# Block-recurrent cross-attention and a cosine-gated feed-forward: moving weight conversion into the middle of a step, evictions to ScalarE, and the order of the first steps

## The chip, the cores and the metric

The kernel runs on one core of a Trainium2 chip. The metric is the device time of one execution in microseconds (us); lower is better. The profiled execution that is quoted below is one of these executions, recorded by the hardware profiler. Its engines are called PE (TensorE), DVE (VectorE), ACT (ScalarE), POOL (GpSimd) and SP (SyncE, which here only issues DMAs).

## The reference, cut to what matters

The inputs are `x` (8, 8, 512, 64), `state` (8, 8, 32, 64), `w_in` (512, 2048) and `w_out` (2048, 512). The two weights arrive as float64, all else as float32.

```
scores  = x @ state.T / 8;  a  = softmax(scores)     # per batch b and head h
xread   = a @ state                                  # (512, 64) per head
scores2 = state @ x.T / 8;  a2 = softmax(scores2)
sread   = a2 @ x                                     # (32, 64) per head
X = concat([xread, sread], axis=2)  ->  (8 * 544, 512), heads side by side
h = X @ w_in                                         # (4352, 2048)
out = (h * cos(h)) @ w_out                           # (4352, 512)
```

## The kernel before

**Steps.** The main loop runs over tiles, one tile a step: for each batch b of 8, sixteen tiles f of 128 hidden columns by 512 tokens, and then sixteen tiles for the state rows of all batches together, 144 steps in all. Step s of batch 0 is called step s below. The order on each engine is the order of the program text, since the schedule is written out by hand (`manual_schedule`); the engines wait for each other's results.

**What a step does.** `hidden(t)` (L440) makes the hidden tile on PE: two products in float32, recorded as four matmul rows of 128x512. The attention output is never formed: `hidden` multiplies the normalised scores `aT` by `sw`, the product of the state and `w_in` ("state products", `products`, L410, one 512-column quarter nt of `w_in` at a time, evicted from PSUM to `sw` by `products_kept`, L415). The state is scaled by 1/2pi, so that the cosine is taken of 2pi h. `gate` (L446, ACT) adds a magic number that rounds, `gate2` (L451, DVE) takes the distance from the rounded value, `gate3` (L456, ACT) does Abs and Sin, `gate4` (L461, DVE) multiplies by h into `g_all` and so frees the PSUM buffer of the hidden tile. There are two such buffers, so `hidden(t+2)` waits for `gate4(t)`. `output` (L583, by `product`, L506) multiplies g by a block of `w_out`, some steps later (`LAG`): tile t-4 in steps below 8, tile t-3 from step 8 on, where two outputs are done in one step.

**The second product in seven parts.** For two batches together `w_out` is used as a 2x2 block matrix with sums and differences (`s1` to `s4`) made on POOL by `blocks` (L774) in steps 15 to 23; sums and differences of g tiles are made by `minus` (L468) on POOL or DVE.

**The weights' conversion.** Each load of 1 MB of float64 (18 of them, 0 to 3 half as large) is converted in six parts (`convert`, L201): "1" and "2" on ACT read the high and the low words (L218, L221), "a" limits from below (L225, DVE), "b" shifts left (L227, DVE), "c" puts in the sign (L230, DVE), "d" adds the low words (L240, POOL) and, from load 4 on, is split into two instructions of 128x512. Part "c" also sends the next load on SP's queue (`fetch`), since the raw words have been read. Conversion i is begun in the step that `conv_at` (L770) gives: parts "1", "2", "a", "b" there, "a" and "b" behind `gate4`; and "c", "d" in the next step between `gate2` and `gate4`. Loads 4, 5, 7, 8, 10, 11 are `w_in`, 6, 9, 12, 13 the upper half of the blocks of `w_out` and 14 to 17 the others; conversions 4 to 12 stand in steps 0 to 8 and 13 to 17 in steps 10 to 14.

**Where the attention stands.** `plan` (L707) puts the attention of batch b+1 into the steps of batch b, in four lists: `x_act` and `x_dve` are worked off between `gate2` and `gate3`, `y_act` and `y_dve` behind `gate4`. `early` places the transposes of x, the scores, the two maxima (`max1`, `max2`), the shift, both exponentials (`exps`), the sums and the norm; `late` the transposes and products of the state's reads, with `keep`. In steps 0 to 15 `plan(0)` places what is left of batch 0, the state products of batch 0, and the attention of batch 1. `late` and `keep` stand in step 3 for batch 0 and in step 14 for batch 1.

**The start.** Before step 0 (L674 to L702) the first loads, batch 0's attention and conversions 0 to 3 are done; seven products of zeros (`warm`, L668) stand behind the scores. `conv_at`, `plan` and `last` in the loop (L800: conversion 3's "cd" in step 0) set the rest.

The lines that set the order in a step:

```
        hidden(t); go(0)                      # PE: the hidden tile, then plan's products
        gate(t); gate2(t); go(1); go(3)       # x_act, x_dve
        if last >= 0: convert(last, "cd")     # of the step before
        if conv >= 0 and not todo[1]: convert(conv, "1")
        gate3(t); ...; gate4(t)
        ...
        if conv >= 0: convert(conv, "2")
        go(4)                                 # y_dve
        if conv >= 0: convert(conv, "ab")
        ...output...
```

Of the kernel before, what the change touches and what calls it, by code (L numbers as in the profile page):

```python
# [10 lines left out]
I32 = mybir.dt.int32  # L11
U32 = mybir.dt.uint32
ALU = mybir.AluOpType
# [10 lines left out]
def kernel(  # L24
# [8 lines left out]
    nc = tc.nc  # L33
# [9 lines left out]
    WC = 512  # L43
# [24 lines left out]
    NH = NF // 2  # L68
# [50 lines left out]
    def load_state(half, queues):  # L119
        b = slice(4 * half, 4 * half + 4)  # L120
        for k in range(NK):
# [11 lines left out]
    acc = [[ops.tile([P, S], F32, name=f"o{m}{ch}") for ch in range(2)]  # L133
           for m in range(2)]
# [16 lines left out]
    HC = WC // 2  # L151
# [49 lines left out]
    def convert(i, parts):  # L201

        if i < len(loads) and f64:
            for p in parts:
                convert_part(i, p)
        if "c" in parts and i not in (1, 2) and i + 3 < N_LOADS:
            fetch(max(i + 4, 6))

    def convert_part(i, p):
        raw, dst = raws[i], loads[i][0]
        bits = dst.bitcast(I32)
        m, w = dst.shape[1:]
        c0 = m * w if i in (2, 3) else 0
        e = low[i % 2][:, c0:c0 + m * w].rearrange("p (m f) -> p m f", m=m)
        if p == "1":
            nc.scalar.activation(dst, raw.bitcast(F32)[:, :, :, 1],  # L218
                                 func=ACTF.Abs)
        elif p == "2":  # L220
            nc.scalar.activation(e, raw.bitcast(U32)[:, :, :, 0],  # L221
                                 func=ACTF.Copy, scale=2.0 ** -51, bias=2.0)
        elif p == "a":
            engine = nc.gpsimd if i == 1 else nc.vector
            engine.tensor_scalar(dst, dst, 2.0 ** -15, None, op0=ALU.max)  # L225
        elif p == "b":
            nc.vector.tensor_scalar(bits, bits, 3, None,  # L227
                                    op0=ALU.logical_shift_left)
        elif p == "c":
            nc.vector.scalar_tensor_tensor(out=bits, in0=raw[:, :, :, 1],  # L230
                                           scalar=-2 ** 31, in1=bits,
                                           op0=ALU.bitwise_and,
                                           op1=ALU.bitwise_xor)
        else:


            n = 1 if i < 4 else 2
            for j in range(n):
                r = slice(m * j // n, m * j // n + m // n)
                nc.gpsimd.tensor_tensor(bits[:, r], bits[:, r],  # L240
                                        e.bitcast(I32)[:, r], op=ALU.add)

# [1 line left out]
    aT_of, sw_of = {}, {}  # L246

    class Attention:
# [163 lines left out]
            self.per_head(stT, lambda rows, k: w_in[rows, k, cols], c1 - c0,  # L412
                          at if bank is None else acc[bank])

        def products_kept(self, nt, bank=None, c0=0, c1=WC):  # L415
            to = at if bank is None else acc[bank]
            if c0 == 0:
                sw_of[self.b, nt] = swp.tile([P, 2, WC], F32, name="sw")
            for j in range(2):
                dst = sw_of[self.b, nt][:, j, c0:c1]  # L420
                if self.b < 2 and (nt, c0) != (0, 0):
                    nc.vector.tensor_copy(dst, to[j][:, 0:c1 - c0])  # L422
                else:
                    nc.scalar.copy(dst, to[j][:, 0:c1 - c0])  # L424

    attn = {}

    def part(b, name, *args):

        if b not in attn:  # L430
            attn[b] = Attention(b)
        getattr(attn[b], name)(*args)
        if (name, args) == ("reads", (1,)) and b + 1 < B:
            load_x(b + 1)
# [5 lines left out]
    def hidden(t):  # L440
        t.hp = hps.tile([P, S], F32, name="h")[:, 0:t.n]
        for i in range(t.kn):
            nc.tensor.matmul(out=t.hp, lhsT=t.lhs(i), rhs=t.rhs(i),  # L443
                             start=(i == 0), stop=(i == t.kn - 1))
# [27 lines left out]
    MAIN, SIDE = 0, 1  # L472
# [195 lines left out]
    def warm(n, to):  # L668

        for _ in range(n):  # L670
            nc.tensor.matmul(out=to, lhsT=zeros[:, 0:P], rhs=zeros, start=True,
                             stop=True)
# [7 lines left out]
    states_kept(0, at[0])  # L680
    a0.all_tokens(3, 4)
    a0.scores()
    warm(7, acc[SIDE][1])
    convert(0, "12ab")
    convert(1, "12a")
    a0.max1()
# [9 lines left out]
    a0.products(0, MAIN, 0, HC)  # L696
    a0.products_kept(0, MAIN, 0, HC)
    convert(3, "12")
    convert(2, "abcd")
    a0.max2()  # L700
    a0.exp2()
    convert(3, "ab")  # L702

# [1 line left out]
    def plan(b):  # L707
        pe, x_act, y_act, x_dve, y_dve = [
            {s: [] for s in range(NF)} for _ in range(5)]

        def prod(s, b, nt, *bank):
            pe[s].append((b, "products", nt) + bank)
            to = x_dve if b < 2 else x_act
            to[s].append((b, "products_kept", nt) + bank)

        def pairs(s, b, name, kept, i):
            pe[s] += [(b, name, i), (b, name, i + 1)]
            x_act[s].append((b, kept, i))
            y_act[s].append((b, kept, i + 1))

        def early(b, s):
            pairs(s[0], b, "tokens", "tokens_kept", 0)
            pairs(s[1], b, "tokens", "tokens_kept", 2)
            pe[s[2]].append((b, "scores"))
            x_dve[s[2]].append((b, "max1"))
            y_dve[s[2]].append((b, "max2"))
            x_dve[s[3]].append((b, "spread1"))
            y_dve[s[3]].append((b, "shift"))
            y_act[s[4]].append((b, "exps"))
            x_dve[s[5]].append((b, "sums"))  # L730
            y_dve[s[5]].append((b, "spread1"))
            x_dve[s[6]].append((b, "norm1"))

        def late(b, s):
            pairs(s[0], b, "turn", "turn_kept", 0)
            pe[s[1]].append((b, "reads", 0))
            pe[s[2]].append((b, "reads", 1))
            x_dve[s[2]].append((b, "keep"))
            if len(s) > 3:
                turned(b, s[3])  # L740

        def turned(b, s):
            pe[s].append((b, "keep2"))
            x_act[s].append((b, "keep3"))


        if b == 0:
            prod(1, 0, 0, SIDE, HC, WC)
            prod(3, 0, 1, SIDE)
            prod(7, 0, 2, SIDE)  # L750
            prod(10, 0, 3, SIDE)
            prod(13, 1, 0, MAIN)
            late(0, (1, 2, 3, 4))
            early(1, (5, 6, 7, 8, 9, 10, 11))
            late(1, (12, 13, 14))
        else:
            bank = (SIDE,) if b == 1 else ()
            if b == 1:
                turned(1, 0)
            prod(0, b, 1, *[MAIN for _ in bank])  # L760
            prod(4, b, 2, *bank)
            prod(9, b, 3, *bank)
            if b + 1 < B:
                prod(14, b + 1, 0)
                early(b + 1, (1 + (b == 1), 2 + (b == 1), 5, 6, 7, 8, 9))
                late(b + 1, (10, 11, 12, 15))
        return pe, x_act, y_act, x_dve, y_dve


    conv_at = {s: 4 + i for i, s in enumerate(  # L770
        (0, 1, 2, 3, 4, 5, 6, 7, 8, 10, 11, 12, 13, 14))}
    conv_at.update({B * NF + 5: N_LOADS, B * NF + 7: N_LOADS + 1})

    def blocks(op, out_, a, b, r):  # L774
        nc.gpsimd.tensor_tensor(out_[:, r], a[:, r], b[:, r], op=op)
# [10 lines left out]
    LAG = 3  # L786

    line = []
    for step, t in enumerate(tiles()):
        s = step % NF  # L790
        if s == 0 and t.b < B:
            steps = plan(t.b)
        todo = [p[s] if t.b < B else [] for p in steps]

        def go(n):
            for p in todo[n]:
                part(*p)

        last, conv = conv_at.get(step - 1, -1), conv_at.get(step, -1)
        if step == 0:  # L800
            last = 3
        if step == B * NF + (0 if f64 else 8):
            fetch(N_LOADS + 2)
        hidden(t)
        go(0)
        if step == 4:
            states(1, acc[SIDE][1])
        gate(t)
        gate2(t)
        go(1)  # L810
        go(3)
        if last >= 0:
            convert(last, "cd")
        if conv >= 0 and not todo[1]:
            convert(conv, "1")
        gate3(t)
        if later:
            later.pop(0)()
        gate4(t)
        if conv >= 0 and todo[1]:  # L820
            convert(conv, "1")
        if t.pair is not None:
            sums(t)
        if step == 5:
            states_kept(1, acc[SIDE][1])
        go(2)
        if conv >= 0:
            convert(conv, "2")
        go(4)
        if conv >= 0:  # L830
            convert(conv, "ab")
        if step in block_at:
            blocks(*block_at[step])
        if t.pair is not None:
            sums2(t)
        while len(line) >= (LAG if step >= NH else LAG + 1):
            output(line.pop(0))
        line.append(t)
    for t in line:
# [31 lines left out]
```

## Time and profile before

| | |
|---|---|
| median of 4 executions | 815.29 us (814.03 to 816.05) |
| profiled execution, its own time | 816.02 us |
| its span | 814.2 us, granted TensorE clock 0.987 on the mean |
| busy: PE, DVE, ACT, POOL | 775.5, 434.8, 398.8, 183.9 us |
| PE busy from 0 to 125 us | 95.2 us of 125 |
| PE busy from 170 to 810 us | 637.2 us of 640 |

A row of the timeline gives the start, the duration, the engine, the line of the kernel, the operation and its operands, and in brackets how long the engine was idle before it and what ended that. An "x4" means that four instructions have been merged. A row of the waits gives the waiting line, the line waited for, the total, how many times, and the longest. A row of windows gives, for a stretch of time, its length, then the busy time and the instructions in brackets of PE, PE's weight loads, DVE, ACT and POOL, the granted PE clock, the share of DMA and the rate.

### The profile page before, as it was taken

Reading aid. Unit: us, or ns where it says so; the run is one execution under the profiler, and the core shown is the slowest. Engines: PE = TensorE matmul, PEld = TensorE weight load, DVE = VectorE, ACT = ScalarE, POOL = GpSimd, SP = SyncE. Lnnn points to the kernel's source line nnn. Section 1 sums busy time; section 2 is a strip of 40 time slices with the busy share of each in tenths; the row PEclk is TensorE's granted clock in tenths of the full one; section 3 lists DMA queues with packets and bytes.
Section 4 is the critical chain, followed back from the end, with each engine's and each line's share of the span. In section 5 each row is a group of like instructions: output and inputs, shape, how many; then the busy total and the mean of one; then the engine's idle time right before and its main releaser. Section 6 shows DMA issues by size and latency. Waiting matters only on the chain.

```text
span 814.2 us, 7602 instructions
## 1 busy us (share of the span) xinstructions
PE 775.5 (95%) x2738; PEld 349.0 (43%) x2738; DVE 434.8 (53%) x671; ACT 398.8 (49%) x644; POOL 183.9 (23%) x135
## 2 busy tenths in 40 slices
PE   7678689999999999999999999999999999999997
PEld 3233234344444443444444344444344444455553
DVE  5789886662354446853365447743554455432431
ACT  3857766553447353645364445644473445322222
POOL 3343257776000000163000000551000003620200
PEclk9999999999999999999999999999999999999999
DMA  8474250011010211020011210120000113100021
GB/s 232 155 207 155 103 155 15 13 27 26 1 26 1 53 26 27 16 63 1 0 27 24 41 26 14 33 46 1 15 12 0 27 26 69 61 1 13 14 39 38
DMA packets 111653, 37.19 MB, mean 46 GB/s; under 512 B 103616, under 2 KB 103616, under 8 KB 111616
## 3 DMA queue, kind: packets, MB, share of 16 engines
q1 hardware_dynamic: 110912, 36.45, 18.5%
q8 instruction: 21, 0.34, 0.2%
q10 hardware_dynamic: 576, 0.13, 0.1%
q0 software_dynamic: 128, 0.13, 0.1%
q14 instruction: 16, 0.13, 0.1%
HBM read 27.79 MB, written 8.91 MB: 45 GB/s over the span
## 4 chain that ended last, share of the span: by engine, by line
PE 79%; DVE 10%; ACT 8%; issue 1%; DMA 1%; POOL 0%; SPq 0%; DVEq 0%; POOLq 0%; ACTq 0%
PE o L508 43%; PE h L443 26%; PE at L295 4%; PE o L625 3%; PE at L382 2%; DVE q L452 2%; ACT q L458 1%; PE at L268 1%; ACT q L457 1%; DVE g_all L464 1%; DVE w_in L225 1%; DVE xT L315 1%; ACT xT L341 1%; DVE aT L359 1%; ACT q L449 1%
## 5 line engine op out<-in xcount | busy, mean ns | idle before, releaser
L443 PE MATMUL h<-aT,sw 128*128 128x512 f32 x512 | 245.7, 603 | 14.9 <-DVE g_all L464 12.2
L508 PE MATMUL o<-g_all,w_out 128*128 128x512 f32 x512 | 237.6, 601 | 4.4 <-DVE sw L422 2.9
L470 POOL TENSOR_TENSOR g_all<-g_all 128x512 f32<-128x512 f32 x80 | 112.1, 1423 | 461.1 <-DVE g_all L464 453.7
L449 ACT ACTIVATE q<-h 128x512 f32<-128x512 f32 (+1 forms) x144 | 82.3, 572 | 271.3 <-PE h L443 271.3
L452 DVE SCALAR_TENSOR_TENSOR q<-q,h 128x512 f32<-128x512 f32 (+1 forms) x144 | 94.3, 655 | 208.3 <-ACT q L449 208.3
L508 PE MATMUL o<-g_all,s 128*128 128x512 f32 x384 | 177.3, 598 | 0.0
L464 DVE TENSOR_TENSOR g_all<-h,q 128x512 f32<-128x512 f32 (+1 forms) x144 | 94.8, 659 | 139.9 <-ACT q L458 139.6
L443 PEld LDWEIGHTS h<-aT,sw 128*128 128x128 f32 x512 | 97.3, 192 | 141.9 <-issue 110.8
L508 PEld LDWEIGHTS o<-g_all,w_out 128*128 128x128 f32 x512 | 93.9, 190 | 127.2 <-issue 120.8
L457 ACT ACTIVATE q<-q 128x512 f32<-128x512 f32 (+1 forms) x144 | 87.8, 610 | 103.1 <-DVE q L452 103.1
L508 PEld LDWEIGHTS o<-g_all,s 128*128 128x128 f32 x384 | 70.4, 190 | 88.4 <-issue 83.3
L458 ACT ACTIVATE q<-q,halfpi 128x512 f32<-128x512 f32 (+1 forms) x144 | 100.8, 700 | 4.5
L240 POOL TENSOR_TENSOR w_out<-w_out,s 128x512 int32<-128x512 int32 x20 | 27.7, 1404 | 85.0 <-DVE w_out L230 73.9
L470 DVE TENSOR_TENSOR g_all<-g_all 128x512 f32<-128x512 f32 x48 | 33.2, 692 | 1.6
L443 PE MATMUL h<-sT,w_in 128*128 128x256 f32 x128 | 30.2, 379 | 0.0
L424 ACT COPY sw<-at 128x512 f32<-128x512 f32 x48 | 25.7, 589 | 9.0 <-PE at L295 9.0
L625 PE MATMUL o<-w_out,g_all 128*128 128x512 f32 x64 | 29.6, 592 | 0.0
L443 PEld LDWEIGHTS h<-sT,w_in 128*128 128x128 f32 x128 | 24.3, 190 | 10.1 <-issue 6.7
L240 POOL TENSOR_TENSOR w_in<-w_in,s 128x512 int32<-128x512 int32 x16 | 21.0, 1330 | 33.3 <-DVE w_in L230 30.1
L514 DVE SCALAR_TENSOR_TENSOR held<-o,held 128x512 f32<-128x512 f32 x40 | 25.5, 683 | 3.7 <-PE o L508 3.7
L295 PE MATMUL at<-w_in,stT 64*32 64x512 f32 x384 | 26.1, 601 | 0.0
L535 DVE STREAM_TRANSPOSE ot<-held 128x512 f32<-128x512 f32 x32 | 22.2, 695 | 0.0
(84 smaller groups left out, 472.2 us busy)
## 6 DMA issues: line engine op xcount, KB each, us to landing
out_dram<-ot SPq DMA_DIRECT2D x136, 64.0 KB, 2.0
x_b<-in_x_dram SPq DMA_DIRECT2D x64, 128.0 KB, 2.9
g_all<-in_moe_w_out_dram SPq DMA_DIRECT2D x8, 1024.0 KB, 5.0
g_all<-in_moe_w_in_dram SPq DMA_DIRECT2D x6, 1024.0 KB, 5.2
g_all<-in_moe_w_in_dram SPq DMA_DIRECT2D x4, 512.0 KB, 5.9
x_b<-in_moe_w_out_dram SPq DMA_DIRECT2D x1, 1024.0 KB, 5.6
xT<-in_moe_w_out_dram SPq DMA_DIRECT2D x1, 1024.0 KB, 7.7
s<-in_state_dram SPq DMA_DIRECT2D x8, 32.0 KB, 7.2
```

The lines of the kernel that those rows point to most:

```text
L240: nc.gpsimd.tensor_tensor(bits[:, r], bits[:, r], e.bitcast(I32)[:, r], op=ALU.add)
L295: nc.tensor.matmul(out=(to or at)[j][Ns * k:Ns * k + Ns, 0:n], lhsT=w[D * j:D * j + D, self.b, Ns * k:Ns * k + Ns], rhs=r(slice(D * j, D * ...
L424: nc.scalar.copy(dst, to[j][:, 0:c1 - c0])
L443: nc.tensor.matmul(out=t.hp, lhsT=t.lhs(i), rhs=t.rhs(i), start=(i == 0), stop=(i == t.kn - 1))
L449: nc.scalar.activation(t.q, t.hp, func=ACTF.Copy, bias=MAGIC)
L452: nc.vector.scalar_tensor_tensor(out=t.q, in0=t.q, scalar=MAGIC, in1=t.hp, op0=ALU.subtract, op1=ALU.subtract)
L457: nc.scalar.activation(t.q, t.q, func=ACTF.Abs)
L458: nc.scalar.activation(t.q, t.q, func=ACTF.Sin, bias=halfpi, scale=-TWO_PI)
L464: nc.vector.tensor_tensor(t.g, t.hp, t.q, op=ALU.mult)
L470: engine.tensor_tensor(out, a, b, op=ALU.subtract)
L508: nc.tensor.matmul(out=acc[bank][ch], lhsT=w[:, i, P * ch:P * ch + P], rhs=g.g, start=(i == 0), stop=(i == NH - 1))
L625: nc.tensor.matmul(out=acc[MAIN][i], lhsT=t.g[:, P * i:P * i + P], rhs=w_out[:, :, t.f, :], start=(n == 0), stop=(n == NF - 1))
```

## The change

- Part "d" of a conversion is one POOL instruction instead of two.
- Parts "a" and "b" move from the end of the step that begins the conversion to the middle of the next step, ahead of "c" and "d" and so ahead of `gate4`. Conversions 2 and 3 are finished before step 0, behind `max2` and the second exponential of batch 0.
- `conv_at` has no conversion in steps 7 and 9 (before: none in step 9), and goes up to step 15.
- `products_kept` evicts on ACT. `products_taken` does so on DVE; it is used for quarters 1 to 3 of batch 1 and for the second half of quarter 0 of batch 0. Quarters 1 to 3 of batch 0 so go from DVE to ACT.
- The hidden tile of step 1 and the second half of quarter 0 of the state products are issued in step 0; between them stand three products of zeros. Ahead of the conversions at the start, ten products of zeros stand in place of seven.
- `max2` moves from behind `gate4`, in the step of the scores, to the step of the exponentials, between `gate2` and `gate4`, for every batch from 1 on.
- The step with two outputs moves from 8 to 16, so that steps 8 to 15 make the output of tile t-4.

```diff
         else:
-            n = 1 if i < 4 else 2
-            for j in range(n):
-                r = slice(m * j // n, m * j // n + m // n)
-                nc.gpsimd.tensor_tensor(bits[:, r], bits[:, r],
-                                        e.bitcast(I32)[:, r], op=ALU.add)
+            nc.gpsimd.tensor_tensor(bits, bits, e.bitcast(I32), op=ALU.add)
...
-        def products_kept(self, nt, bank=None, c0=0, c1=WC):
+        def products_kept(self, nt, bank=None, c0=0, c1=WC, copy=None):
...
             for j in range(2):
-                dst = sw_of[self.b, nt][:, j, c0:c1]
-                if self.b < 2 and (nt, c0) != (0, 0):
-                    nc.vector.tensor_copy(dst, to[j][:, 0:c1 - c0])
-                else:
-                    nc.scalar.copy(dst, to[j][:, 0:c1 - c0])
+                (copy or nc.scalar.copy)(sw_of[self.b, nt][:, j, c0:c1],
+                                         to[j][:, 0:c1 - c0])
+
+        def products_taken(self, *args):
+            self.products_kept(*args, copy=nc.vector.tensor_copy)
...
-    warm(7, acc[SIDE][1])
+    warm(10, acc[SIDE][1])
...
     convert(3, "12")
-    convert(2, "abcd")
     a0.max2()
     a0.exp2()
-    convert(3, "ab")
+    convert(2, "abcd")
+    convert(3, "abcd")
...
             pe[s].append((b, "products", nt) + bank)
-            to = x_dve if b < 2 else x_act
-            to[s].append((b, "products_kept", nt) + bank)
+            if b == 1 and nt > 0:
+                x_dve[s].append((b, "products_taken", nt) + bank)
+            else:
+                x_act[s].append((b, "products_kept", nt) + bank)
...
             x_dve[s[2]].append((b, "max1"))
-            y_dve[s[2]].append((b, "max2"))
             x_dve[s[3]].append((b, "spread1"))
             y_dve[s[3]].append((b, "shift"))
+            x_dve[s[4]].append((b, "max2"))
             y_act[s[4]].append((b, "exps"))
...
         if b == 0:
-            prod(1, 0, 0, SIDE, HC, WC)
+            pe[0].append((0, "products", 0, SIDE, HC, WC))
+            y_dve[0].append((0, "products_taken", 0, SIDE, HC, WC))
...
     conv_at = {s: 4 + i for i, s in enumerate(
-        (0, 1, 2, 3, 4, 5, 6, 7, 8, 10, 11, 12, 13, 14))}
+        (0, 1, 2, 3, 4, 5, 6, 8, 10, 11, 12, 13, 14, 15))}
...
-        if step == 0:
-            last = 3
...
-        hidden(t)
+        if step != 1:
+            hidden(t)
+        if step == 0:
+            hidden(all_tiles[1])
+            warm(3, acc[MAIN][0])
         go(0)
...
         if last >= 0:
-            convert(last, "cd")
+            convert(last, "abcd")
...
         go(4)
-        if conv >= 0:
-            convert(conv, "ab")
...
-        while len(line) >= (LAG if step >= NH else LAG + 1):
+        while len(line) >= (LAG if step >= 2 * NH else LAG + 1):
             output(line.pop(0))
```

More of the change, by code (lines that the diff above doesn't have):

```diff
@@ L788 @@
     line = []
-    for step, t in enumerate(tiles()):
+    all_tiles = list(tiles())
+    for step, t in enumerate(all_tiles):
         s = step % NF
```

## The prediction

> **What bounds the kernel now.** First the page's slices, then the same by stages in the view of windows, then PE's waits. The page:
>
> ```profile
> PE   7678689999999999999999999999999999999997
> DVE  5789886662354446853365447743554455432431
> PEclk9999999999999999999999999999999999999999
> ```
>
> Stretches of time (length, then busy PE, PE loads, DVE, ACT, POOL; granted clock; DMA):
>
> ```profile
> 21.00:33.00 12.00, 7.90 (x48) 3.19 (x32) 8.23 (x16) 9.39 (x17) 2.52 (x2) 0.86 0.49 167
> 33.00:48.50 15.50, 12.23 (x60) 4.94 (x61) 13.94 (x21) 11.69 (x15) 5.93 (x4) 0.89 0.49 153
> 48.50:75.00 26.50, 21.98 (x90) 10.02 (x89) 24.65 (x28) 19.36 (x27) 12.00 (x9) 0.94 0.61 189
> 75.00:100.00 25.00, 18.86 (x61) 7.33 (x59) 20.97 (x31) 16.27 (x24) 6.53 (x6) 1.00 0.35 126
> 100.00:125.00 25.00, 19.35 (x94) 7.57 (x95) 22.40 (x28) 16.79 (x25) 11.64 (x9) 0.93 0.44 127
> 170.00:814.20 644.20, 637.18 (x2181) 290.13 (x2179) 302.63 (x488) 291.23 (x487) 103.47 (x73) 1.00 0.13 25
> ```
>
> From 170 us on PE is full (637.2 of 640 to 810 us), and the change neither adds nor removes PE work there. Only steps 0 to 16 (21 to 126 us) can give or take time: PE is busy 80.3 of 104 us, DVE 90.2, ACT 73.5. DVE is the fullest. PE waited there for, among others:
>
> ```profile
> PE h L443 <- DVE g_all L464: 8.9, 6, 2.5
> PE o L295 <- POOL w_in L240: 7.8, 4, 3.1
> PE o L508 <- DVE sw L422: 2.9, 1, 2.9
> ```
>
> So PE waits for gate4 (the end of DVE's turn), for POOL's "d" ahead of state products, and for an eviction. Why DVE is so full is seen in the timeline, at conversions 8 and 11:
>
> ```profile
> 54.81 2.52 POOL L240 TENSOR_TENSOR w_in<-w_in,s 128x512 int32<-128x512 int32 x2 [2.43 <-DVE w_in L230]
> 56.05 1.83 DVE L225 TENSOR_SCALAR w_in<-w_in 128x1024 f32<-128x1024 f32 x1 [0.37 <-ACT w_in L218]
> 57.91 0.69 DVE L227 TENSOR_SCALAR w_in<-w_in 128x1024 int32<-128x1024 int32 x1
> 76.47 0.68 DVE L225 TENSOR_SCALAR w_in<-w_in 128x1024 f32<-128x1024 f32 x1
> 77.19 0.69 DVE L227 TENSOR_SCALAR w_in<-w_in 128x1024 int32<-128x1024 int32 x1
> ```
>
> "a" takes 0.68 us alone and 1.83 when it meets POOL's "d": it ends 0.55 us after the second half of "d" (57.33).
>
> **Prices.** *Conversion.* Of 28 "a" and "b" in steps 0 to 14, nine "a" take 1.05 to 1.83 (12.75 in all, 6.6 above 0.68) and seven "b" 1.64 to 1.66 (11.5 in all, 6.7 above 0.69): 13.3 us of DVE lost. Moved to the next mid-step, a conversion costs DVE 0.72 + 0.74 + 1.11 = 2.6 us between gate2 and gate4 (spacing of the rows at 67.37, 68.10 and 79.55 to 80.66). Abs and Sin on ACT take 0.66 + 0.72 = 1.4 in that time, so gate4 comes 1.2 us later after its gate2 than now; in return the next gate2 can follow at once, where now up to 3.4 us of "a" and "b" stand ahead of it.
>
> *Part "d" in one instruction.* No row of this operation has 1024 elements; the f32 sums of 128x1024 in `blocks` take 2.37, the two halves 2.51 undisturbed. Undisturbed it lies between 2.37 and 2.51, disturbed halves take up to 3.06 (row at 106.59); I take 2.4, the nearest in size. What only needs the first half waits 1.2 us longer: output(0) in step 4 (now it starts at 50.77, behind the first half) and quarter 1 of the state products.
>
> *Evictions.* Three pairs at 1.28 leave DVE (3.8 us) and cost ACT 1.1 each (row of L424, two copies).
>
> *Zero products.* Seven took 6.28 us up to 17.47; ten end at about 20.05, and the product they stand ahead of waits for POOL until 20.55: hidden. They fill the idle stretch after which PE ran at half clock (hidden tiles 0 and 1: 5.40 us instead of 8 x 0.43 = 3.44). The three in step 0 (2.6 us) end at 27.9, when "d" of conversion 3 is due at 27.8: hidden; at half clock they would cost 2.6. hidden(1) stands there before too in effect (both run in one row of eight), so its earlier issue is worth nothing. Conversions 2 and 3 behind max2 let ACT's second exponential start at 23.1 for 24.7, and conversion 3's "d" end at 27.8 for 29.4.
>
> *max2* (1.5 us) in the step of the exponentials: in the row at 154.33 gate2 is done at 155.0, so max2 at 156.6; Sin ends at 156.43, the second exponential starts at 158.71. Nothing waits; gate4 is 0.1 later, and hidden has 1 us to spare. Zero for batches 2 to 7; in step 9 it delays "d" of conversion 11 by 1.5.
>
> *The second output* moves from step 8 to 16: 1.72 us of PE leave a stage with idle PE and return where it is full. It is inside the sum below, since both sides have then done the same outputs. SP's queue: by the reckoning below every load is read 6.8 us or more after its issue, against a landing of 5.0 to 6.0: free; "c" moves no load behind another.
>
> **The sum.** I lay out both DVE and ACT by hand with these spacings: gate to gate2 0.62, gate2 to next 0.60, conversion 2.6, gate4 to next 0.60; on ACT Abs to Sin 0.66, Sin to next 0.63, "1" and "2" 1.05 each; on PE hidden and output 1.72, products and reads 1.09. Start of gate2, before (rows of L452) and as reckoned:
>
> - step 0: 26.7 and 26.4; step 2: 38.3 and 36.6; step 3: 43.65 and 40.5. "a" and "b" no longer stand ahead of gate2.
> - step 3 loses most of it: quarter 1 waits for "d" of conversion 5 (42.3), its copies on ACT at 44.3 hold Abs back; the reads end at 45.8, `keep` and conversion 6 follow, gate4 at 49.6 (before 49.3).
> - step 4: 52.85 and 50.2; then output(0) waits for "d" of conversion 6 until 52.2 and hidden(5) ends at 55.8: step 5 58.5 and 56.5.
> - step 7: 69.7 and 67.2; step 8: 77.8 and 72.2; step 9: 84.6 and 76.2. Steps 7 and 9 begin no conversion, max2 is out of step 7: 8.4 us ahead.
> - step 9: max2, then conversion 11: its "d" ends at 83.3. Quarter 3 in step 10 waits for it (PE idle 5 us), ACT's Abs waits for the copies until 85.1: steps 10 and 11 start at 82.4 and 90.4 (before 90.9 and 98.1).
> - step 12: 104.6 and 96.0; output(8) waits for "d" of conversion 12 until 97.5. From there PE is full: 15.3 us of PE to hidden(16), five hidden, four outputs, reads and products.
> - steps 15 and 16: POOL has "d" of conversion 16 (to 119.7) and the first `blocks` sum (to 122.1) back to back. Conversion 17's "a" or "b", due at 119.6, has to wait for the sum as at 56.05: about 2.6 us, and gate4(16) ends at 125.5.
>
> hidden(18) starts then; before, it is this row:
>
> ```profile
> 129.92 1.88 PE L443 MATMUL h<-aT,sw 128*128 128x512 f32 x4
> ```
>
> That is 4.4 us ahead, with PE full behind it and the same stall at 164.8 us to come. Half-clock stretches come off: before, PE ran at half clock after waits such as
>
> ```profile
> 101.73 1.98 PE L443 MATMUL h<-aT,sw 128*128 128x512 f32 x4 [1.94 <-DVE g_all L464]
> 120.05 2.48 PE L443 MATMUL h<-aT,sw 128*128 128x512 f32 x4 [2.45 <-DVE g_all L464]
> ```
>
> where 1.94 us of idling left 1.98 for four and 2.45 led to 2.48. A stretch takes about 1.7 us of PE work (2 us lost in the 5.40 above). After the change the waits in steps 4 (3.5 us), 10 (5.0) and 12 (5.5) would each bring one. In step 12 it costs 1.0 (the rest is swallowed by the wait for gate4(16)), in step 4 0.7 (1.4, likely every other time), in step 10 nothing that lasts. 4.4 - 1.0 - 0.7 = 2.7 us: 816.0 - 2.7 = 813.3 on the profiled execution. This stood 0.7 above the median, so 812.6 against 815.3.
>
> **Rules weighed against rows.** The Trainium skill, "SBUF — State Buffer", Who interferes with whom, holds the ports that DVE and GpSimd share to be locked for a whole instruction, the later one blocked; a merged "d" then locks longer. By it the collision in step 16 costs its full 2.6, as the rows gave; if the engines shared the ports smoothly, the sum would be near 5. The Trainium skill, "TensorE: Matmul & The Clock Gate", The HAM clock gate, names an idle window of about 3.4 us before the clock falls; the 2.45 us above disagree, and the rows decide. By the page step 4's wait counts too, and the sum would be 2.0.
>
> **Rivals.** *ACT becomes the bound (slower).* Place: Abs behind the copies in steps 3 and 10. For: ACT gains 3.5 us and holds Abs 3.1 and 2.0 us for PE and POOL, 8.6 together. Against: ACT now idles 25.4 us for gate2 in 12 waits, which should shrink. It decides where they shrink by less than 8.6; at 5 the kernel is 3.6 slower, 819; at none 824.
>
> *The waits for "d" eat it all (no change).* With both half-clock stretches in full (1.7 + 1.4) and one more collision like step 16's (1.2), 4.4 becomes 0.1: 815. For it: the new waits of PE for POOL (4.4, 3.5, 5.0, 5.5) are longer than the present 7.8 + 1.5.
>
> *The stage keeps its lead.* Where the collision in step 16 and the half clock don't bite, hidden(17) at 119.4 against 126.5 leaves 7.1, and 8.4 if step 9's lead is all kept: 807 to 808.
>
> **How the numbers follow.** Forecast (1.7 to 5 us faster, 810.3 to 813.6): 0.43. Larger gain: 0.17. No change: 0.18. Slower: 0.22. About 0.2% (1.6 us) is what a measurement of this kernel can tell from no change. So faster 0.60, same 0.18, slower 0.22. The range goes from the larger gain to the nearer half of the slower rival: 807.0 to 818.0.
>
> **What would show it.** In the profile after: "a" and "b" at 0.7 but for steps 4, 12, 15 and 16; one POOL row of 2.4 a conversion; hidden 0 and 1 in 3.4 us; gate2 of step 9 before 79; PE's waits for L240 above 15 us; hidden(18) at 125 to 128; from there equal lengths. Wrong, if Abs waits for copies more than for gate2, if "a" meets "d" in most steps, or if the length behind hidden(18) changes.

## The result and the profile after

The changed kernel takes 817.41 us (median of 39 executions, 815.52 to 819.26), the kernel before 815.61 (63 executions). The ratio is 1.0023, 95% interval 1.0019 to 1.0028: slower by 1.8 us, where 2.7 us faster was forecast. The profiled execution took 818.37 us with a span of 816.6. Lines shift by 6: the hidden product is L437, gate L443, gate2 L446, Abs and Sin L451 and L452, gate4 L458, output L502, the state products L289, "d" L235, the block sums L772; "a", "b", "c" stay L225, L227, L230.

The page after:

```profile
PE   8769699989999999999999999999999999999997
DVE  5768776662355435853464447743554355432531
PEclk9989899999999999999999999999999999999999
```

The stages (length, then busy PE, PE loads, DVE, ACT, POOL; granted clock; DMA):

```profile
21.00:33.00 12.00, 10.21 (x58) 4.42 (x42) 8.95 (x16) 9.67 (x17) 2.60 (x2) 1.00 0.44 167
33.00:48.50 15.50, 10.05 (x59) 4.36 (x58) 10.37 (x17) 11.41 (x17) 4.73 (x2) 0.89 0.49 154
48.50:75.00 26.50, 22.09 (x91) 10.00 (x89) 20.95 (x28) 19.40 (x28) 10.02 (x5) 0.94 0.63 188
75.00:100.00 25.00, 17.64 (x52) 6.97 (x52) 18.67 (x28) 19.33 (x28) 5.44 (x3) 0.86 0.26 85
100.00:125.00 25.00, 23.89 (x105) 10.23 (x106) 19.81 (x29) 18.59 (x26) 10.23 (x5) 0.93 0.61 167
170.00:810.00 640.00, 637.62 (x2183) 290.46 (x2182) 304.58 (x490) 290.56 (x488) 104.29 (x72) 1.00 0.13 24
```

DVE was relieved, as it should be: 78.8 us in these 104 (the sum of the first five rows) for 90.2. But the clock is at 0.86 to 0.94 from 33 us on, and lower than before in 75 to 100 us (1.00 then). Behind 170 us nothing has changed.

PE's waits from 21 to 136 us, then the rows that decide:

```profile
PE o L289 <- POOL w_in L235: 9.2, 3, 4.6
PE o L502 <- POOL w_out L235: 7.9, 2, 4.1
PE h L437 <- DVE g_all L458: 3.7, 3, 2.0
```

```profile
42.99 1.93 PE L289 MATMUL o<-w_in,stT 64*32 64x512 f32 x8 [4.10 <-POOL w_in L235]
...
53.18 3.66 PE L502 MATMUL o<-g_all,w_out 128*128 128x512 f32 x4 [4.06 <-POOL w_out L235]
...
85.93 1.93 PE L289 MATMUL o<-w_in,stT 64*32 64x512 f32 x8 [4.60 <-POOL w_in L235]
87.79 3.42 PE L502 MATMUL o<-g_all,w_out 128*128 128x512 f32 x4
...
101.09 3.60 PE L502 MATMUL o<-g_all,w_out 128*128 128x512 f32 x4 [3.85 <-POOL w_out L235]
...
125.21 2.79 POOL L772 TENSOR_TENSOR s<-w_out 128x1024 f32<-128x1024 f32 x1
125.83 2.72 DVE L227 TENSOR_SCALAR w_out<-w_out 128x1024 int32<-128x1024 int32 x1
...
130.66 2.81 PE L437 MATMUL h<-aT,sw 128*128 128x512 f32 x4 [2.01 <-DVE g_all L458]
```

The waits for POOL's "d" in step 4 (4.06 us) and step 12 (3.85) are each followed by an output at half speed: 3.66 and 3.60 us for what takes 1.9 elsewhere. The waits in steps 3 (4.10) and 10 (4.60) are followed by eight product rows in 1.93 us, for 1.06 at full speed, and in step 10 by an output of 3.42. In step 16 "b" of conversion 17 meets the first block sum and takes 2.72 us in place of 0.69; gate4 is late, PE waits 2.01, and hidden(18) again runs partly at half speed. It starts at 130.66, where 125.5 was reckoned and 129.92 was the time before.

### The profile page after: what moved, and what is told of

Read it like the earlier page. It is cut to its first block, busy times and chain, and to the rows that moved or that the text cites. A ratio compares the mean times of both kernels' runs of the same rounds, so it can differ in the third digit from the quotient of the medians.

```text
span 816.6 us, 7612 instructions
## 1 busy us (share of the span) xinstructions
PE 780.7 (96%) x2750; PEld 352.4 (43%) x2750; DVE 425.3 (52%) x665; ACT 401.4 (49%) x650; POOL 178.7 (22%) x119
## 4 chain that ended last, share of the span: by engine, by line
PE 79%; DVE 10%; ACT 7%; POOL 1%; DMA 1%; issue 1%; SPq 0%; DVEq 0%; POOLq 0%
PE o L502 43%; PE h L437 25%; PE at L289 3%; PE o L619 3%; PE at L376 2%; DVE q L446 2%; PE at L262 1%; ACT q L452 1%; ACT q L451 1%; DVE aT L353 1%; DVE g_all L458 1%; ACT q L443 1%; ACT s L221 1%; ACT L452 1%; DVE w_out L230 1%; PE o L289 1%
## 5 line engine op out<-in xcount | busy, mean ns | idle before, releaser
L437 PE MATMUL h<-aT,sw 128*128 128x512 f32 x512 | 242.4, 596 | 9.8 <-DVE g_all L458 8.0
L502 PE MATMUL o<-g_all,w_out 128*128 128x512 f32 x512 | 241.3, 609 | 7.9 <-POOL w_out L235 7.9
L443 ACT ACTIVATE q<-h 128x512 f32<-128x512 f32 (+1 forms) x144 | 82.2, 571 | 278.3 <-PE h L437 278.1
L446 DVE SCALAR_TENSOR_TENSOR q<-q,h 128x512 f32<-128x512 f32 (+1 forms) x144 | 94.3, 655 | 226.8 <-ACT q L443 226.6
L502 PE MATMUL o<-g_all,s 128*128 128x512 f32 x384 | 177.3, 598 | 0.0
L458 DVE TENSOR_TENSOR g_all<-h,q 128x512 f32<-128x512 f32 (+1 forms) x144 | 94.8, 658 | 132.1 <-ACT q L452 131.3
L437 PEld LDWEIGHTS h<-aT,sw 128*128 128x128 f32 x512 | 96.9, 191 | 135.1 <-issue 110.4
L502 PEld LDWEIGHTS o<-g_all,w_out 128*128 128x128 f32 x512 | 95.4, 193 | 132.1 <-issue 119.3
L451 ACT ACTIVATE q<-q 128x512 f32<-128x512 f32 (+1 forms) x144 | 87.6, 608 | 89.3 <-DVE q L446 89.3
L502 PEld LDWEIGHTS o<-g_all,s 128*128 128x128 f32 x384 | 70.3, 190 | 88.4 <-issue 84.4
L452 ACT ACTIVATE q<-q,halfpi 128x512 f32<-128x512 f32 (+1 forms) x144 | 100.5, 698 | 4.5
L235 POOL TENSOR_TENSOR w_out<-w_out,s 128x1024 int32<-128x1024 int32 x10 | 23.9, 2385 | 89.9 <-DVE w_out L230 89.9
L437 PE MATMUL h<-sT,w_in 128*128 128x256 f32 x128 | 30.2, 379 | 0.0
L437 PEld LDWEIGHTS h<-sT,w_in 128*128 128x128 f32 x128 | 24.3, 190 | 10.1 <-issue 6.2
L235 POOL TENSOR_TENSOR w_in<-w_in,s 128x1024 int32<-128x1024 int32 (+1 forms) x10 | 19.3, 1930 | 37.4 <-DVE w_in L230 27.3
L289 PE MATMUL at<-w_in,stT 64*32 64x512 f32 x384 | 26.1, 601 | 0.0
```

Source lines behind the costliest of these rows:

```text
L235: nc.gpsimd.tensor_tensor(bits, bits, e.bitcast(I32), op=ALU.add)
L289: nc.tensor.matmul(out=(to or at)[j][Ns * k:Ns * k + Ns, 0:n], lhsT=w[D * j:D * j + D, self.b, Ns * k:Ns * k + Ns], rhs=r(slice(D * j, D * ...
L437: nc.tensor.matmul(out=t.hp, lhsT=t.lhs(i), rhs=t.rhs(i), start=(i == 0), stop=(i == t.kn - 1))
L443: nc.scalar.activation(t.q, t.hp, func=ACTF.Copy, bias=MAGIC)
L446: nc.vector.scalar_tensor_tensor(out=t.q, in0=t.q, scalar=MAGIC, in1=t.hp, op0=ALU.subtract, op1=ALU.subtract)
L451: nc.scalar.activation(t.q, t.q, func=ACTF.Abs)
```

## The experiments

Theory A: the lead is real, and it is lost to the waits for "d", to the half clock behind them, and to the collision in step 16. Rival B: ACT has become the bound, since Abs stands behind evictions that wait for PE. All ratios are to the kernel before, run on the same chip at the same time, and most are good to about 0.001, or 1 us. Differences from the changed kernel in microseconds are between medians of different sessions; the ratios give the same to 0.3 us.

### The conversions' steps as before

```diff
-        (0, 1, 2, 3, 4, 5, 6, 8, 10, 11, 12, 13, 14, 15))}
+        (0, 1, 2, 3, 4, 5, 6, 7, 8, 10, 11, 12, 13, 14))}
```

> The changed kernel with the conversions 11 to 17 begun in steps 7, 8, 10 to 14 again, as before the change. Theory A (PE's waits for POOL's part d, the half clock behind them, and the collision of conversion 17 with the first block sum cost the lead): the waits in steps 10 (4.6 us) and 12 (3.9 us) go, conversion 17 is done in step 15, ahead of the block sum, so the 2.7 us row of the shift left goes; DVE has 2.6 us more in steps 8 and 9. Expected 811 to 813.5, ratio to the kernel before 0.995 to 0.998. Rival B (evictions on ACT hold Abs back): nothing of this matters, 816.5 to 818.

Measured: 812.79 us, ratio 0.9968 (0.9957 to 0.9980). PE's waits from 21 to 136 us in this run:

```profile
PE h L437 <- DVE g_all L458: 11.2, 7, 2.9
PE o L289 <- POOL w_in L235: 4.1, 1, 4.1
PE o L502 <- POOL w_out L235: 3.4, 1, 3.4
```

The waits of steps 10 and 12 are gone and only those of steps 3 (4.1) and 4 (3.4) are left for "d"; "b" of conversion 17 takes 0.69 us again. DVE is fuller, so gate4 is waited for more (11.2 for 3.7 us), and still the kernel is 4.6 us faster than the changed one. As theory A has it.

### The first block sum one step later

```diff
-    block_at = {15: (ALU.add, s1, a21, a22, lo),
+    block_at = {16: (ALU.add, s1, a21, a22, lo),
```

> The changed kernel with the first block sum in step 16 instead of 15, so that it no longer runs on POOL while conversion 17's limit and shift are due on DVE. Theory A: the shift takes 0.7 instead of 2.72 us, PE's wait of 2.0 us for gate4 of step 16 and the half clock behind it (1.7 us) go: 813 to 815, ratio 0.997 to 0.999. Rival B: no change from the changed kernel, 817.4.

Measured: 814.39 us, ratio 0.9984 (0.9976 to 0.9993). Timeline of this run, the same "b" and hidden(18):

```profile
125.67 0.69 DVE L227 TENSOR_SCALAR w_out<-w_out 128x1024 int32<-128x1024 int32 x1
...
128.48 1.98 PE L437 MATMUL h<-aT,sw 128*128 128x512 f32 x4
```

One instruction on POOL, moved by a step, is worth 3.0 us in the medians. The two profiled executions are 3.9 us apart: 2.2 by hidden(18) (128.48 for 130.66) and 1.7 behind it, where the half clock is gone.

### Products thrown away in the waits

```diff
             warm(3, acc[MAIN][0])
+        if step in (3, 10):
+            warm(4 if step == 3 else 5, acc[SIDE][0])
         go(0)
...
+        if step in (4, 12):
+            warm(4, acc[MAIN if step == 4 else SIDE][0])
         while len(line) >= (LAG if step >= 2 * NH else LAG + 1):
```

> The changed kernel with products that are thrown away put into PE's waits in steps 3 (4), 4 (4), 10 (5) and 12 (4), into banks that the next product overwrites. They shorten no wait, they only keep PE busy. Theory A: the half clock behind those waits goes, 1.7 us of PE work each in steps 4 and 12, about 1 in steps 3 and 10; the collision in step 16 stays and swallows part: 812.5 to 815.5. If the half clock is of no weight (the wait alone counts): 817 to 818. Rival B: 817 to 818.

Measured: 812.60 us, ratio 0.9963 (0.9951 to 0.9975). Windows around the waits of steps 3, 4 and 10, the changed kernel first, then this run:

```profile
40.00:58.00 18.00, 10.95 (x41) 5.16 (x42) 12.42 (x18) 9.49 (x14) 6.88 (x3) 0.81 0.70 190
82.00:94.00 12.00, 8.07 (x19) 3.00 (x20) 6.23 (x10) 9.06 (x16) 2.35 (x1) 0.72 0.28 87
```

```profile
40.00:58.00 18.00, 16.69 (x74) 7.46 (x73) 14.39 (x22) 11.91 (x19) 7.07 (x3) 1.00 0.79 230
82.00:94.00 12.00, 11.69 (x43) 5.40 (x40) 7.99 (x12) 10.37 (x15) 0.40 (x1) 1.00 0.21 81
```

And two rows of its timeline, output(0) and hidden(18):

```profile
51.44 1.98 PE L502 MATMUL o<-g_all,w_out 128*128 128x512 f32 x4 [0.64 <-POOL w_out L235]
...
126.42 1.98 PE L437 MATMUL h<-aT,sw 128*128 128x512 f32 x4 [2.02 <-DVE g_all L458]
```

The clock goes from 0.81 and 0.72 to 1.00, and work that computes nothing makes the kernel 4.8 us faster. This run also sizes the half clock wait by wait, as the start of gate2 (us). The reckoned time of step 13 isn't on record; it is worked out here from the recorded 97.5 of output(8), with two turns of 1.72 on PE and 0.62 to gate2:

| step | before | reckoned | changed | with the fill |
|---|---|---|---|---|
| 3 | 43.65 | 40.5 | 41.0 | 40.9 |
| 4 | 52.85 | 50.2 | 51.3 | 49.5 |
| 5 | 58.5 | 56.5 | 59.2 | 55.8 |
| 9 | 84.6 | 76.2 | 78.7 | 75.2 |
| 11 | 98.1 | 90.4 | 94.1 | 89.8 |
| 13 | 110.1 | 101.6 | 107.1 | 102.8 |
| hidden(18) | 129.9 | 125.5 | 130.7 | 126.4 |

From the last two columns, less the 0.15 us by which the two were apart already in step 3: 1.6 us are lost in step 3, another 1.7 in step 4, 0.9 in step 10, 4.1 in all by hidden(18). In step 12 the two differ by nothing, since there the clock fell in the filled kernel too. Behind hidden(18) the spans differ by a further 1.6 us (685.9 and 684.4 to the end), although that wait was not filled. So these two executions are 5.8 us apart, and the medians 4.8.

### The evictions back on DVE

```diff
-            if b == 1 and nt > 0:
+            if b < 2 and (b, nt) != (1, 0):
                 x_dve[s].append((b, "products_taken", nt) + bank)
```

> The changed kernel with quarters 1 to 3 of batch 0's state products evicted on DVE again. Rival B: Abs in steps 3, 7 and 10 is no longer behind copies that wait for PE; 813 to 815. Theory A: ACT is not what ends last, DVE gets 3.8 us back; 817.5 to 819.5.

Measured: 817.82 us, ratio 1.0026 (1.0016 to 1.0037): the same as the changed kernel. ACT's waits from 21 to 126 us, first the longest of the kernel before, then the changed kernel's, then this run's:

```profile
ACT q L457 <- DVE q L452: 25.4, 12, 4.2
```

```profile
ACT sw L414 <- PE o L289: 10.9, 4, 4.0
ACT q L451 <- DVE q L446: 10.2, 10, 1.9
ACT q L443 <- PE h L437: 6.8, 4, 3.1
```

```profile
ACT q L443 <- PE h L437: 14.1, 6, 5.5
ACT q L451 <- DVE q L446: 11.6, 11, 1.9
ACT sw L414 <- PE o L289: 4.0, 2, 3.5
```

ACT's wait for the copies' data only turns into a wait for the next hidden tile. What it waits for is the same late PE. Rival B falls.

### Both mends, and the conversions with the fill

The fill of all four waits together with the later block sum:

> The changed kernel with both mends that worked singly: thrown-away products in the waits of steps 3, 4, 10 and 12, and the first block sum in step 16. The waits for part d themselves stay. Theory A with effects that add: 817.4 less 4.8 less 3.0, some of it shared: 809.5 to 811. If the two mend the same loss: 812.5, as the fill alone.

Measured: 809.66 us, ratio 0.9935 (0.9922 to 0.9947). From the changed kernel's 1.0023 that is 0.0088; the two alone gave 0.0060 and 0.0039. They add up but for 0.0011, which is within the intervals: two losses and not one.

The conversions' steps as before, with the fill in steps 3 and 4 alone:

> The changed kernel with the conversions' steps as before the change and thrown-away products in the waits of steps 3 and 4, which that version still has. Theory A: the fill saves up to 1.7 us on top of the 812.8 of the conversions alone: 810.5 to 812.5. If only where conversions stand counts: 812.8.

Measured: 809.16 us, ratio 0.9923 (0.9911 to 0.9936), the clock 1.00 from 21 to 170 us. It beats both kernels, and the fill is worth 0.0045 on top of the 0.9968 of the conversions. That is 3.6 us, twice the 1.7 that was expected at most: from 100 to 125 us, where nothing is filled, the granted clock is 1.00 as well, against 0.86 without the fill. Ahead of the hidden tile of step 16, PE waits 2.9 us in both runs; the tile then takes 3.78 us without the fill and 1.98 with it. Whether that is the fill's doing or chance was not tried.

### One part alone: limit and shift in mid-step

In the kernel before (its step 0 keeps "c" and "d" of conversion 3):

```diff
-            convert(last, "cd")
+            convert(last, "cd" if step == 0 else "abcd")
...
-        if conv >= 0:
-            convert(conv, "ab")
```

> The kernel before with one part of the change: limit and shift in the middle of the next step, ahead of the sign. DVE is relieved of most of the 13.3 us of blocking by part d, ahead of gate4 stand 1.4 us more. If the gain that the prediction saw is in this part: 811 to 813.5. If DVE's relief is worth nothing without the other parts: 815 to 817.

Measured: 810.78 us, ratio 0.9944 (0.9931 to 0.9956). hidden(18) in its timeline, at 129.92 before:

```profile
124.30 1.88 PE L443 MATMUL h<-aT,sw 128*128 128x512 f32 x4
```

So this one move gives 4.4 us, and all the other parts of the change together take 6.6 us away again (1.0023 for 0.9944).

### The same with the later conversions

The kernel of the last run with `conv_at` of the change:

> The kernel before with limit and shift in mid-step (810.8 alone) and, in addition, the changed kernel's steps for the conversions (none in 7 and 9, the last in 15). Theory A: the later conversions alone take the gain back, through the wait of an output for conversion 12, and conversion 17 colliding with the first block sum: 814 to 819. If the later conversions only hurt together with the other parts: 810 to 812.5.

Measured: 821.74 us, ratio 1.0081 (1.0069 to 1.0093). Timeline, output(8) and hidden(18):

```profile
98.40 3.56 PE L508 MATMUL o<-g_all,w_out 128*128 128x512 f32 x4 [7.17 <-POOL w_out L240]
...
132.71 3.47 PE L443 MATMUL h<-aT,sw 128*128 128x512 f32 x4 [3.70 <-DVE g_all L464]
```

The later conversions alone cost 11 us here, more than was expected. output(8) stands in step 11, one step earlier than in the changed kernel, waits 7.17 us for conversion 12 with the next hidden tile behind it, and then runs at half speed; in step 16 PE waits 3.70 us for the collision, and again at half speed. In the changed kernel the later conversions cost 4.6 us. That it is less there because the second output comes later is likely, but not shown: other parts differ too.

### Part "d" in two halves again

In the changed kernel, the removed loop over halves is put back.

> The changed kernel with part d in two halves again. output(0) in step 4 and output(8) in step 12 need only the first half and can start 1.2 us earlier, so the waits of 4.1 and 3.9 us shrink, while a half clock may still follow them. If the length of d counts: 815 to 816.5. If only the half clock behind the waits and the collision count: 817 to 818.

Measured: 815.04 us, ratio 0.9994 (0.9985 to 1.0003), 2.4 us less than the changed kernel. output(0) in its timeline:

```profile
51.64 3.55 PE L506 MATMUL o<-g_all,w_out 128*128 128x512 f32 x4 [2.98 <-POOL w_out L238]
```

It starts 1.5 us earlier (51.64 for 53.18), still at half clock. In step 12 the wait didn't shrink: output(8) waits 4.19 us, for 3.85. The two profiled executions are 3.9 us apart, half of it by hidden(18) (128.71 for 130.66) and half behind it: the collision stayed (PE waits 2.03 us for gate4 of step 16), but in this profile no half clock followed it. How much of the 2.4 us is due to the halves themselves isn't settled by these rows.

The version with the earlier conversions, the fill and the halves:

> The conversions' steps as before, the thrown-away products in steps 3 and 4 (809.2 together), and part d in halves again. Step 4's output(0) starts 1.2 us earlier, elsewhere DVE can slip between the halves: 808 to 809.2. If nothing waits for the first half alone any more: 809 to 810.

Measured: 808.10 us, ratio 0.9924 (0.9908 to 0.9941): no difference to 0.9923 with the merged "d" that six executions can tell (807.65 to 812.05 us). It fits that PE waits only 0.7 us in all for "d" from 21 to 136 us: where the waits are filled and the conversions early, hardly anything waits for the first half.

### The fill in the kernel before

```diff
         hidden(t)
+        if step in (3, 6):
+            warm(3, acc[SIDE][0])
         go(0)
```

> The kernel before with three thrown-away products each in its own waits of steps 3 and 6, behind which PE ran at half clock. If the half clock weighs there as in the changed kernel: 1 to 3 us faster, 812.5 to 814.5. If behind those waits DVE ends last anyway, so that a slow PE is hidden: 815 to 816.

Measured: 814.90 us, ratio 0.9994 (0.9985 to 1.0003): no change that can be told, though up to 1.2 us lies within the interval. Windows of this run:

```profile
33.00:48.50 15.50, 13.45 (x67) 5.43 (x67) 14.82 (x23) 12.25 (x17) 5.93 (x4) 1.00 0.54 170
48.50:75.00 26.50, 24.31 (x96) 10.74 (x97) 24.59 (x28) 19.56 (x27) 11.73 (x9) 1.00 0.61 187
```

The clock is 1.00 where it was 0.89 and 0.94. In step 6 nothing is gained: the output and the hidden tile behind the wait take 1.88 us each for 2.92 and 2.58, and gate2 of step 7 still starts at 69.95, for 69.68 before, since DVE is busy 24.6 of 26.5 us there and ends last. In step 3 a little is. The evictions there, before and in this run:

```profile
45.19 1.29 DVE L422 COPY sw<-o 128x512 f32<-128x512 f32 x2 [0.86 <-PE o L295]
```

```profile
45.47 1.29 DVE L422 COPY sw<-o 128x512 f32<-128x512 f32 x2
```

DVE had waited 0.86 us for the slow products, and that wait is gone. This execution had come 1.2 us later to step 3 (gate2 at 44.81 for 43.65), so the two profiles end alike. Of the 3.2 us that the half clock took from PE in these two places (1.45 and 1.74 by the rows), at most 0.9 reached DVE: the half clock was nearly free as long as DVE was the bound.

## Why the prediction was wrong

- **The bound and the main gain: right.** DVE's blocked "a" and "b" filled the first stage, and moving them gives 4.4 us alone. That the same 4.4 was reckoned for the whole change at hidden(18) is chance, since that sum had the later conversions in it. Blocked rows are left in steps 4, 12, 15 and 16, the four that were named ("a" 1.81, 1.34, 1.82, "b" 2.72 us), and once more ahead of step 0 ("b" of conversion 3, 1.39), which was not foreseen.
- **The hand layout: right to about 1 us.** With the clock kept up in three of the four waits, hidden(18) starts at 126.42, against 125.5 reckoned with no half clock. The waits were named with their sizes: step 3 4.4 (measured 4.10), step 4 3.5 (4.06), step 10 5.0 (4.6), step 12 5.5 (3.85). Two slips in its words don't touch the sum: the 15.3 us up to hidden(16) hold three hidden tiles and not five (seven turns of 1.72 and three of 1.09), and the most that "a" and "b" take ahead of a gate2 is 3.1 us in the rows and not 3.4.
- **The half clock: the step that failed.** "In step 12 it costs 1.0 [...], in step 4 0.7 [...], in step 10 nothing that lasts". For the waits of steps 3, 4, 10 and 16 together 0.7 us was priced; the two profiled executions with and without the fill show 5.7: 1.6 in step 3, whose wait was named but given no half clock, 1.7 in step 4, 0.9 in step 10, and 1.6 behind hidden(18), where the collision was priced but no half clock after it. These 5.0 us are nearly the whole distance of 5.1 from the forecast (2.7 faster) to the profiled execution (2.4 slower); of the medians' distance of 4.5, the fill gives back 4.8. For step 12 the 1.0 may be right: the filled kernel kept the half clock there, and its hidden(18) is 0.9 behind the 125.5. The size of one stretch, 1.7 us, was right as well. What failed was which waits bring one, and the reasoning that other waits swallow it: the run on the kernel before shows this to hold there but for 0.9 us at most, and the change took away the full DVE that did the swallowing.
- **Luck in it.** Behind hidden(18) the half clock came in the changed kernel (2.81 us) and in the run with the evictions on DVE (2.69), not in those with the fill and with the halves (1.98), after the same wait of 2.0 us. So this 1.6 us is in part the luck of an execution; the changed kernel's times spread from 815.52 to 819.26.
- **The rule on the idle window.** Discounting step 4's wait as "likely every other time" left the size to chance; the page's window of about 3.4 us (the Trainium skill, "TensorE: Matmul & The Clock Gate", The HAM clock gate) would have counted it in full, though the sum would have been 2.0 us faster even so. Waits of 2.0 us were followed by half speed as well (the row at 130.66) and in another run not (126.42), so the page's length is no safe lower limit here.
- **The port lock.** The collision cost 2.03 us of DVE ("b" 2.72 for 0.69), a little less than the reckoned 2.6; DVE waited until the sum was done, as "SBUF — State Buffer", Who interferes with whom, has it for the engine that comes second.
- **The conversions' steps: a term with the wrong sign.** That steps 7 and 9 begin no conversion was booked as part of the lead in step 9. Undone, it gives 4.6 us; alone on the mid-step version it costs 11. The later "d" of conversions 11, 12 and 17 is what the waits in steps 10 and 12 and the collision are made of; I priced each wait, but never set their sum against the alternative. The half clock behind those waits is in these figures too, so they overlap with the 5.7 us above.
- **ACT as the bound: wrong rival, by its own condition.** ACT's waits for gate2 shrank from 25.4 to 10.2 us, by 15.2 and so by more than the 8.6 that it named, and the run with the evictions back on DVE changed nothing. "The waits for d eat it all" was the nearest, but it too counted only two stretches of half clock and ended at no change.
- **The signs of being wrong.** Two of the three came true: the copies on ACT, which stand ahead of Abs, waited 10.9 us, a little more than the 10.2 for gate2, and the length behind hidden(18) grew from 684.3 to 685.9 us. The first one misled, since moving the evictions back gave nothing. "a" did not meet "d" in most steps.
- **Costed at nothing and found so:** ten products of zeros (the product behind them starts at 20.70 for 20.61, the hidden tiles 0 and 1 take 3.70 for 5.40 us) and the DMA order (none of ACT's waits from 21 to 126 us is for a load). max2 in the later step, the second output in step 16 and the earlier hidden tile were not tried by themselves.

## What to carry to other kernels

Price a wait of the matmul engine by its length and by the slow stretch behind it, and ask what else is late at that moment: here the half clock was nearly free while another engine ended last, and most of it was paid once that engine had been relieved. When work on a full engine is put off to later steps, follow its consumers one by one: here an output four steps on and a sum on POOL were the price. A wait that can't be removed can be filled with products whose result is overwritten; that gave 0.6% for four lines, and nothing that could be measured in the kernel where DVE was the bound.

## What the runs showed of the hardware

- A wait of 2.0 us can be enough for the half clock (hidden(18) at 130.66: 2.81 us for four rows), and the same wait in another run has none behind it (126.42: 1.98). In step 12, 1.87 us of waiting led to an output of 3.23 us in the run with the fill and to one of 1.98 in the run with both mends:

```profile
96.76 3.23 PE L502 MATMUL o<-g_all,w_out 128*128 128x512 f32 x4 [1.87 <-POOL w_out L235]
```

```profile
97.72 1.98 PE L502 MATMUL o<-g_all,w_out 128*128 128x512 f32 x4 [1.87 <-POOL w_out L235]
```

In the kernel before, a wait of 2.90 us (output at 92.34, 1.96 us) had none behind it. A length alone doesn't tell.

- Waits of 3.0 to 7.2 us were followed by outputs of 3.55 to 3.66 us for four rows (four such rows above, in three kernels), for 1.9 otherwise.
- DVE's shift waited 2.0 us for a POOL sum of 2.79; the POOL sum itself takes 2.37 us otherwise, and began while DVE's limit (125.05 to 125.80) was still running. Both engines lost in this meeting.
